# Attention parts in a written order on four engines: one change to the overlapped mLSTM and MLP kernel

## The chip, the cores and the metric

The kernel runs on one core of one Trainium2 chip. The metric is the device time of one execution in microseconds, the median of three runs. The profile is of one further execution. Engine names: PE is TensorE, ACT is ScalarE, DVE is VectorE, POOL is GpSimd, and SP is the engine whose queue triggers the DMAs.

## The reference, cut to what matters

An mLSTM layer (4 batches, 8 heads, 768 positions, head size 40) is followed by two two-layer MLPs over the same 3072 tokens (320 to 2048 to 320), the first with a squared ReLU, the second with SiLU. Everything is float32.

```python
for t in range(S):
    m_new = np.maximum(f_gate[:, :, t] + m, i_gate[:, :, t])
    f_stab = np.exp(f_gate[:, :, t] + m - m_new)
    i_stab = np.exp(i_gate[:, :, t] - m_new)
    C = f_stab * C + i_stab * np.einsum('bhd,bhe->bhde', vt, kt)
    n = f_stab * n + i_stab * kt
    h_tilde = np.einsum('bhde,bhe->bhd', C, qt)
    y[:, :, t] = sigmoid(o_gate) * h_tilde / np.maximum(np.abs(n . qt), 1.0)
x = relu(y @ w1_in) ** 2 @ w1_out
h = x @ w2_in
out = (h * sigmoid(h)) @ w2_out
```

## The kernel before

**Attention.** The recurrence is done in chunks of 128 positions, all 8 heads together. One chunk of one batch is a *tile*, and there are 24, numbered i. Tiles 0 to 5 use a simpler form (`i < N_NAT`); the others split their numbers into parts that TensorE multiplies exactly. A tile's work: `load_a`, `load_w`, `load_e` start the DMAs (q and k, v, the decay matrix W, the row factors eq); `SK` copies q and k on ACT into `tt`, `SK2` subtracts on DVE and issues nine DMAs `stk<-tt` (lines 286 and 288) that stack the parts on partitions; `WT` masks W on POOL and takes its exponentials on ACT, eight ACTIVATEs; `SC(i, hf)` multiplies q and k for one half of the heads on PE into a PSUM tile, then multiplies by W and makes the parts p1, p2, p3 on DVE (lines 320, 326, 327); `QT` scales q and splits it into qh (ACT) and ql (DVE); `VK` splits v and k on DVE; `HG` is the output product on PE, 48 small matmuls and nine for the carried state; `EV` normalises it on DVE; `ST` makes the new state on PE, then adds and splits it on DVE and ACT (`cs`); `xt` transposes the result on PE and writes x on ACT (line 467) and DVE (line 468).

**MLP one** runs over blocks of 384 tokens, three tiles each, eight blocks. A block has 16 steps (`KF`). Step j does `emit_in` for step j+3 (8 matmuls `hin`, line 530, then relu and two squares on ACT, lines 537, 538, 540, and later `gl` on DVE, line 549) and `emit_out` for step j (8 matmuls into three PSUM tiles). The PSUM tiles of `hin` are two, so the `hin` of one step needs the relu of the one two earlier. After step 15 the block's output goes through `ob` (ACT, DVE, ACT, lines 573 to 575) and a DMA (line 576) to DRAM. MLP two is alike and has no attention beside it.

**Overlap.** The attention tiles of block n+1 are done during block n (and the last six steps of the one before). `plan(i)` gives every part of tile i a moment in steps, relative to `b = base(i)`, the start of its score product; three tiles are 5.33 steps apart, at 10, 15.33 and 20.67 counted from the start of a block. A moment is rounded down to half a step: `run_events(slot)` emits the parts of the first half between `emit_in` and `emit_out`, those of the second half after `emit_out`. In the same places the weights of MLP two are decoded (`w_load`, `w_dec`, then a store to DRAM), one of 16 pieces every six steps. Raw weights, decoded weights and `ob` share two buffers with the tag `raw`.

**Order.** PE executes in the order in which the code emits. For ACT, DVE, POOL and the SP queue the order is found by a scheduler, which takes instructions as they come ready in its own model of time, and starts from the emitted order as a priority. Every engine and the queue then executes in the order given to it: an instruction that waits holds those behind it.

Of the kernel before, what the change touches and what calls it, by code (L numbers as in the profile page):

```python
# [22 lines left out]
L = 128  # L23
# [37 lines left out]
def mlstm_moe_kernel(  # L61
# [104 lines left out]
    def w_split(raw, which, layer, u, pl):  # L166
# [3 lines left out]
        act.activation(out=f(t), in_=f(hi), func=ACTF.Prelu, scale=2.0 ** -112, alpha=-2.0 ** 32)  # L170
        dve.tensor_scalar(out=t, in0=t, scalar1=3, scalar2=None, op0=ALU.logical_shift_left)
        dve.scalar_tensor_tensor(out=t, in0=lo, scalar=29, in1=t,
                                 op0=ALU.logical_shift_right, op1=ALU.bitwise_or)
        if which == "i":
# [7 lines left out]
            act.activation(out=w[:, 0:3], in_=tv, func=ACTF.Copy)  # L182
            eng = pool if layer == 1 else dve
            eng.tensor_tensor(out=w[:, 3:5], in0=tv[:, 0:2], in1=f(w[:, 0:2]), op=ALU.subtract)
            eng.tensor_tensor(out=w[64:128, 2], in0=tv[64:128, 2], in1=f(w[64:128, 2]), op=ALU.subtract)
        else:
            if layer == 1:
                w = wp.tile([128, 2, 640], F32R, tag=f"wo{u}", name=f"wo{u}")
                wout[layer, u] = w
            else:  # L190
                ws = pl.tile([128, 1280], F32R, tag="raw", name="ws")
                w = ws.rearrange("p (j n) -> p j n", j=2)
            tv = f(t).rearrange("p (j n) -> p j n", j=2)
            if layer == 1:
                for c, oh, ol in ((slice(0, 256), slice(0, 256), slice(256, 512)),
                                  (slice(256, 320), slice(512, 576), slice(576, 640))):
                    act.activation(out=w[:, :, oh], in_=tv[:, :, c], func=ACTF.Copy)
                    pool.tensor_tensor(out=w[:, :, ol], in0=tv[:, :, c], in1=f(w[:, :, oh]), op=ALU.subtract)
                return
            oh, ol = w[:, :, 0:320], w[:, :, 320:640]  # L200
            act.activation(out=oh, in_=tv, func=ACTF.Copy)
            dve.tensor_tensor(out=ol, in0=tv, in1=f(oh), op=ALU.subtract)
        if layer == 2:
            raws["st", which, u] = lambda: sp.dma_start(out=w2_d[which, u], in_=f(ws))
# [20 lines left out]
    def load_a(i):  # L225
# [12 lines left out]
        v = d["vk"] = at.tile([128, DM + 2 * VW], F32, tag="vk", name="vk", bufs=2)  # L238
        sp.dma_start(out=v[:, 0:DM + VW], in_=vk[i * L:(i + 1) * L])

    def load_s(n):
        t0, nt = blk_tiles[n]
        sg = T["sg", n] = at.tile([128, 3, DM], F32, tag="sg", name="sg", bufs=1)
        sp.dma_start(out=sg[:, 0:nt], in_=og[t0 * L:(t0 + nt) * L].rearrange("(k p) f -> p k f", p=L))
        act.activation(out=sg[:, 0:nt], in_=sg[:, 0:nt], func=ACTF.Sigmoid)
# [45 lines left out]
    def WT(i, hf):  # L291
        b, c = TILES[i]
        w = T[i]["W", hf]
        pool.affine_select(out=w, in_=w, pattern=[[0, 4], [1, L]], compare_op=ALU.is_ge,  # L294
                           fill=NEG, base=0, channel_multiplier=-1)
        r0 = b * H + 4 * hf
        for h in range(4):
            act.activation(out=w[:, h], in_=w[:, h], func=ACTF.Exp, bias=aw[:, 0, c, r0 + h:r0 + h + 1])  # L298

    def SC(i, hf):  # L300
# [5 lines left out]
        for h in range(4):  # L306
            if i < N_NAT:
# [6 lines left out]
                      start=True, stop=True)  # L314
        w = d["W", hf]
# [12 lines left out]

    def VK(i):
        b, c = TILES[i]  # L330
        d = T[i]
        vkt = d["vk"]
        k, v, r = vkt[:, 0:DM], vkt[:, DM:DM + VW], vkt[:, DM + VW:DM + 2 * VW]
# [5 lines left out]
        dve.tensor_tensor(out=r, in0=v, in1=top(v), op=ALU.subtract)  # L339
        v3 = at.tile([128, VW], BF16, tag="v3", name="v3", bufs=2)  # L340
        dve.tensor_tensor(out=v3, in0=r, in1=top(r), op=ALU.subtract)
        d["v"] = [x.rearrange("p (h c) -> p h c", c=42) for x in (top(v), top(r), v3)]
# [13 lines left out]
    def QT(i):  # L356
# [6 lines left out]
        (pool if i < N_NAT else dve).tensor_tensor(out=q, in0=q, in1=eqv(i)[0:120], op=ALU.mult)  # L363
        if i < N_NAT:
            return
        act.activation(out=qh[0:120], in_=q, func=ACTF.Copy)
        dve.tensor_tensor(out=ql[0:120], in0=q, in1=f(qh[0:120]), op=ALU.subtract)
# [50 lines left out]
    def ST(i):  # L418
# [3 lines left out]
        cv = cc2[b % 2][0:120]  # L422
        cs = cs2[b % 2][0:120]
        mv = bmask[0:120, 0:H].to_broadcast([120, H, 42])

        def grow(h0, h1, m, src):
            dve.scalar_tensor_tensor(out=cv[0:m, h0:h1], in0=cv[0:m, h0:h1],
                                     scalar=eqv(i)[0:m, h0 // 3, L - 1:L], in1=src, op0=ALU.mult, op1=ALU.add)

        ps = p_at.tile([128, 512], F32, tag="at", name="st")[:, 0:VW].rearrange("p (h c) -> p h c", c=42)  # L430
        if i < N_NAT:
            vkt = T[i]["vk"]
            ks, vp, pairs = [vkt], [vkt[:, DM:DM + VW].rearrange("p (h c) -> p h c", c=42)], ((0, 0),)
        else:
            ks, vp, pairs = T[i]["k"], T[i]["v"], PAIRS
        for h in (0, 3, 6):
            n = min(3, H - h)
            for m, (x, y) in enumerate(pairs):
                pe.matmul(ps[0:40 * n, h:h + n], ks[x][:, 40 * h:40 * h + 40 * n], vp[y][:, h:h + n],
                          start=m == 0, stop=m == len(pairs) - 1)  # L440
        if c == 0:
            act.activation(out=cv[:, 0:6], in_=ps[0:120, 0:6], func=ACTF.Copy)
            act.activation(out=cv[0:80, 6:8], in_=ps[0:80, 6:8], func=ACTF.Copy)
        else:
            for h in (0, 3, 6):
                n = min(3, H - h)
                grow(h, h + n, 40 * n, ps[0:40 * n, h:h + n])
# [350 lines left out]
```

## Time and profile before

| what | us |
|---|---|
| median of 3 runs | 919.86 |
| the three runs | 915.72, 919.86, 926.69 |
| the profiled execution | 918.51 |
| its span, first to last instruction | 916.8 |
| PE busy in the span | 860.2 |
| DVE busy | 513.4 |
| ACT busy | 515.5 |

PE is busy nearly all the time, ACT and DVE a little over half. A busy PE is not one at its peak, since matmuls overlap. The first `emit_out` of the eight blocks of MLP one starts at 74.3, 152.5, 220.7, 282.3, 344.5, 408.4, 472.7 and 525.2 us; MLP two begins near 570. Blocks two to seven, the ones in the change's name, are 152.5 to 525.2.

### The profile page before, as it was taken

To read this page: it belongs to the slowest core of one execution; us is meant where nothing else is said; L and a number is where in the kernel's file an instruction comes from. 1 tells how busy PE (TensorE), PEld (TensorE's weight loads), DVE (VectorE), ACT (ScalarE), POOL (GpSimd) and SP (SyncE) were. 2 spreads that over 40 slices of the span, in tenths; PEclk is the share of its full clock that TensorE was granted. 3 is DMA by queue.
4 is the path that set the end of the run, shared out by engine and by line. 5 is a ranking of instruction groups with operands and counts; after the bars stand their busy time and mean duration, and the time that the engine had idled before them with its cause. 6 is when DMAs were issued, how large, how long until landed. Compare 5 with 4: busy or idle time off the path is not lost.

```text
span 916.8 us, 15812 instructions
## 1 busy us (share of the span) xinstructions
PE 860.2 (94%) x5964; PEld 839.9 (92%) x5964; DVE 513.4 (56%) x1001; ACT 515.5 (56%) x1071; POOL 94.6 (10%) x121
## 2 busy tenths in 40 slices
PE   3868979898899899899999999999999999999998
PEld 3758979898899899899999999999999999999998
DVE  5576476866656877778666323443444444444443
ACT  3677556766686686768675655343434344343343
POOL 4675200000000100000000000000000000000000
PEclk9997999989999999999899999999999999999999
DMA  8794355656846647657444477010101010000000
GB/s 244 240 281 151 108 168 166 231 157 182 247 147 205 208 124 253 196 170 243 146 135 151 144 247 248 11 57 1 57 1 56 1 57 1 23 1 22 1 22 23
DMA packets 72582, 117.50 MB, mean 128 GB/s; under 512 B 5306, under 2 KB 54394, under 8 KB 72266
## 3 DMA queue, kind: packets, MB, share of 16 engines
q1 hardware_dynamic: 72506, 116.50, 40.3%
q8 instruction: 47, 0.77, 0.4%
q14 instruction: 29, 0.24, 0.1%
HBM read 77.23 MB, written 19.33 MB: 105 GB/s over the span
## 4 chain that ended last, share of the span: by engine, by line
PE 62%; DMA 15%; ACT 8%; DVE 7%; SPq 4%; issue 2%; POOL 1%; POOLq 0%; ACTq 0%; DVEq 0%
PE hin L530 29%; DMA W<-g_d 8%; PE o L582 6%; PE o L580 6%; PE o L581 6%; ACT W L298 3%; DMA eq<-e_d 3%; PE o L563 2%; PE o L565 2%; PE o L564 2%; SPq L288 2%; PE hA L401 2%; DVE gl L549 1%; DMA stk<-tt 1%; PE o L568 1%
## 5 line engine op out<-in xcount | busy, mean ns | idle before, releaser
L530 PE MATMUL hin<-x,wi 128*128 128x384 f32 x2048 | 417.5, 346 | 14.7 <-ACT r L537 7.6
L530 PEld LDWEIGHTS hin<-x,wi 128*128 128x128 f32 x2048 | 366.1, 192 | 19.9 <-ACT r L537 10.1
L549 DVE TENSOR_TENSOR gl<-r,gh 128x384 fp32r<-128x384 f32 x256 | 147.3, 577 | 131.1 <-ACT gh L546 68.9
L545 DVE TENSOR_TENSOR r<-hin,r 128x384 f32<-128x384 f32 x128 | 71.4, 558 | 121.9 <-ACT r L544 121.8
L544 ACT ACTIVATE r<-hin 128x384 f32<-128x384 f32 x128 | 63.0, 492 | 131.7 <-PE hin L530 131.6
L582 PE MATMUL o<-wo,gl 128*128 128x320 f32 x384 | 118.7, 309 | 0.0
L580 PE MATMUL o<-wo,gh 128*128 128x320 f32 x384 | 118.3, 308 | 0.0
L581 PE MATMUL o<-wo,gh 128*128 128x320 f32 x384 | 117.8, 307 | 0.0
L546 ACT ACTIVATE gh<-r 128x384 fp32r<-128x384 f32 x128 | 67.3, 526 | 73.9 <-DVE r L545 73.9
L563 PE MATMUL o<-gh,wo 128*128 128x384 f32 x256 | 91.8, 359 | 3.9 <-ACT ob L573 3.9
L565 PE MATMUL o<-gl,wo 128*128 128x384 f32 x256 | 87.5, 342 | 2.3 <-DVE gl L549 2.3
L537 ACT ACTIVATE r<-hin 128x384 f32<-128x384 f32 x128 | 61.6, 481 | 48.7 <-PE hin L530 48.4
L564 PE MATMUL o<-gh,wo 128*128 128x384 f32 x256 | 87.6, 342 | 0.0
L581 PEld LDWEIGHTS o<-wo,gh 128*128 128x128 f32 x384 | 72.1, 188 | 0.0
L580 PEld LDWEIGHTS o<-wo,gh 128*128 128x128 f32 x384 | 72.1, 188 | 0.0
L582 PEld LDWEIGHTS o<-wo,gl 128*128 128x128 f32 x384 | 72.0, 187 | 0.0
L294 POOL TENSOR_SCALAR_AFFINE_SELECT W<-W 128x512 f32<-128x512 f32 x48 | 35.7, 768 | 346.8 <-DMA W<-g_d 129.9
L298 ACT ACTIVATE W<-W,aw 128x128 f32<-128x128 f32 x192 | 60.9, 390 | 18.0 <-POOL W L294 17.9
L538 ACT ACTIVATE gh<-r 128x384 fp32r<-128x384 f32 x128 | 67.0, 524 | 2.7
L540 ACT ACTIVATE r<-r 128x384 f32<-128x384 f32 x128 | 66.8, 522 | 2.6
L563 PEld LDWEIGHTS o<-gh,wo 128*128 128x128 f32 x256 | 49.6, 194 | 5.5 <-ACT ob L573 4.3
L565 PEld LDWEIGHTS o<-gl,wo 128*128 128x128 f32 x256 | 49.0, 191 | 3.0 <-DVE gl L549 3.0
(124 smaller groups left out, 1191.6 us busy)
## 6 DMA issues: line engine op xcount, KB each, us to landing
stk<-tt SPq DMA_DIRECT2D x162, 120.0 KB
raw<-in_w_in_dram SPq DMA_DIRECT2D x16, 768.0 KB
W<-g_d SPq DMA_DIRECT2D x24, 512.0 KB
raw<-in_w_out_dram SPq DMA_DIRECT2D x16, 640.0 KB
vk<-in_vk_dram SPq DMA_DIRECT2D x24, 328.0 KB
rqk<-in_qk_dram SPq DMA_DIRECT2D x18, 360.0 KB
w2i_d<-ws SPq DMA_DIRECT2D x8, 640.0 KB
w2o_d<-ws SPq DMA_DIRECT2D x8, 640.0 KB
```

The costliest lines, as they stand in the source:

```text
L298: act.activation(out=w[:, h], in_=w[:, h], func=ACTF.Exp, bias=aw[:, 0, c, r0 + h:r0 + h + 1])
L530: pe.matmul(ps[:, 0:N], w[:, c, ws], x[:, sl, 0:N], start=(k == 0), stop=(k == 7))
L538: act.activation(out=gh, in_=r, func=ACTF.Square)
L545: dve.tensor_tensor(out=g, in0=ps[:, 0:N], in1=r, op=ALU.mult)
L546: act.activation(out=gh, in_=g, func=ACTF.Copy)
L549: low.append(lambda: on("gl" if ly == 1 else "gl2", gi).tensor_tensor(out=gl, in0=g, in1=f(gh), op=ALU.subtract))
L563: pe.matmul(o[k][:, 0:N], w[:, c], gh, start=first, stop=False)
L564: pe.matmul(o[k][:, 0:N], w[:, c2], gh, start=False, stop=False)
L565: pe.matmul(o[k][:, 0:N], w[:, c], gl, start=False, stop=last)
L580: pe.matmul(o[k][:, 0:DM], gh[:, c], w[:, 0:320], start=first, stop=False)
L581: pe.matmul(o[k][:, 0:DM], gh[:, c], w[:, 320:640], start=False, stop=False)
L582: pe.matmul(o[k][:, 0:DM], gl[:, c], w[:, 0:320], start=False, stop=last)
```

## The change

`plan(i)` now has 26 parts where there were 14 (and the sigmoid load, which becomes two). Most functions that used two engines are divided: `load_a` into `load_q` and `load_v`, `WT` into `WT` (POOL) and `WE` (ACT), `SC` into `SC` (PE) and `SD` (DVE), `VK` into `VV` and `VK`, `QT` into `QT`, `QH`, `QL`, `ST` into `ST`, `GR`, `CH`, `CL`, and `xt` into `XT`, `XA`, `XL`. The weight decoding becomes a generator whose five pieces are called at five moments, after each tile's `b` instead of every six steps. From the start of block two to the start of block eight the emitted order holds for ACT, DVE and the SP queue as it does for PE; POOL keeps the scheduler's order. The instructions themselves are the same.

```diff
+    def WE(i, hf):
+        b, c = TILES[i]
+        w = T[i]["W", hf]
         r0 = b * H + 4 * hf
         for h in range(4):
             act.activation(out=w[:, h], in_=w[:, h], func=ACTF.Exp, bias=aw[:, 0, c, r0 + h:r0 + h + 1])
...
+    def SD(i, hf):
+        d = T[i]
+        ps = d["sc", hf]
...
         def plan(i):
             b = base(i)
             p = base(i - 2) if i >= nb0 + 2 else -20.0
-            todo = [(b - 6.3, lambda: load_a(i)), (max(b - 5.5, p + 3.6), lambda: load_w(i)),
-                    (max(b - 3.6, p + 4.8), lambda: load_e(i)), (b - 4.2, lambda: SK(i)), (b - 3.4, lambda: SK2(i)),
-                    (b - 2.0, lambda: (WT(i, 0), WT(i, 1))), (b - 0.4, lambda: VK(i)),
-                    (b, lambda: SC(i, 0)), (b + 0.5, lambda: SC(i, 1)), (b + 0.6, lambda: QT(i)),
-                    (b + 3.2, lambda: (HG(i, 0), HG(i, 1), HG(i, 2))), (b + 3.9, lambda: EV(i)),
-                    (b + 4.6, lambda: ST(i)), (b + 6.4, lambda: xt(i))]
+            e = KF * (i // 3) - AHEAD
+            q0 = max(b - 8.0, p + (1.2 if i < N_NAT else 2.4))
+            todo = [(q0, lambda: load_q(i)), (max(b - 5.0, p + 4.8), lambda: load_v(i)),
+                    (max(b - 6.4, p + 3.8), lambda: load_w(i)), (max(b - 4.6, p + 5.5), lambda: load_e(i)),
+                    (max(b - 4.4, q0 + 0.6), lambda: SK(i)), (max(b - 3.7, q0 + 1.2), lambda: SK2(i)),
+                    (b - 2.4, lambda: WT(i, 0)), (b - 2.3, lambda: WT(i, 1)),
+                    (b - 1.8, lambda: WE(i, 0)), (b - 1.2, lambda: WE(i, 1)), (b - 1.5, lambda: VV(i)),
+                    (b, lambda: SC(i, 0)), (b + 0.5, lambda: SD(i, 0)), (b + 0.9, lambda: QT(i)),
+                    (b + 1.0, lambda: SC(i, 1)), (b + 1.4, lambda: QH(i)), (b + 1.5, lambda: SD(i, 1)),
+                    (b + 2.2, lambda: QL(i)), (b + 2.6, lambda: VK(i)),
+                    (b + 3.3, lambda: (HG(i, 0), HG(i, 1), HG(i, 2))), (b + 3.9, lambda: EV(i)),
+                    (b + 4.4, lambda: ST(i)), (b + 4.9, lambda: GR(i)), (b + 5.4, lambda: CH(i)),
+                    (b + 6.1, lambda: CL(i)),
+                    (min(b + 6.1, e - 1.6), lambda: XT(i)), (min(b + 6.6, e - 1.1), lambda: XA(i)),
+                    (min(b + 6.9, e - 0.6), lambda: XL(i))]
             if i % 3 == 0:
-                todo.append((b - 1.0, lambda: load_s(i // 3)))
+                todo.append((b - 0.9, lambda: load_s(i // 3)))
+                todo.append((b + 1.5, lambda: sig(i // 3)))
...
-            for at_, fn in ((17.0, lambda e=e: w_load(2, e, stp)), (19.0, lambda e=e: w_dec(2, e, stp)),
-                            (21.5, lambda e=e: raws.pop(("st", *e))())):
-                events.setdefault(int(2 * (at_ + 6 * k)), []).append((at_ + 6 * k, fn))
+            dec = []
+            b = base(6 + k)
+            fns = [(b + 1.0, lambda e=e: w_load(2, e, stp)),
+                   (b + 3.0, lambda e=e, dec=dec: (dec.append(w_dec(2, e, stp)), next(dec[0])))]
+            fns += [(b + x, lambda dec=dec: next(dec[0], None)) for x in (3.6, 4.4, 5.1, 6.5)]
+            for at_, fn in fns:
+                events.setdefault(int(2 * at_), []).append((at_, fn))
...
-        with tc.manual_schedule(engines={nc.tensor.engine}):
+        with ExitStack() as order:
+            order.enter_context(tc.manual_schedule(engines={pe.engine}))
...
+                if ly == 1 and n in (1, nb1 - 1):
+                    order.close()
+                    order.enter_context(tc.manual_schedule(
+                        engines={pe.engine, act.engine, dve.engine, sp.engine} if n == 1 else {pe.engine}))
```

## Rows read from the trace of the kernel before

**Rows 1.** Busy time by stretch: blocks one to eight of MLP one, each from its first `emit_out` to the next block's. Columns: stretch and its length, busy us (and instructions) of PE, PE's weight loads, DVE, ACT and POOL, mean granted PE clock, DMA share, GB/s.

```profile
74.30:152.50 78.20, 72.06 (x477) 68.06 (x476) 47.26 (x101) 48.77 (x107) 17.30 (x19) 0.93 0.43 131
...
282.30:344.50 62.20, 58.96 (x507) 56.33 (x506) 46.41 (x100) 44.20 (x99) 4.74 (x6) 1.00 0.61 186
344.50:408.40 63.90, 60.73 (x518) 59.25 (x516) 48.33 (x107) 45.25 (x98) 4.17 (x6) 0.97 0.62 201
408.40:472.70 64.30, 62.12 (x518) 60.67 (x515) 46.39 (x101) 44.82 (x98) 4.58 (x6) 0.95 0.56 181
220.70:282.30 61.60, 57.91 (x470) 55.98 (x470) 42.96 (x87) 45.40 (x99) 4.45 (x6) 0.97 0.60 186
152.50:220.70 68.20, 61.89 (x515) 60.15 (x515) 47.50 (x104) 45.80 (x100) 4.42 (x6) 0.95 0.61 199
472.70:525.20 52.50, 51.74 (x387) 50.35 (x386) 28.93 (x57) 31.53 (x62) 2.12 (x2) 1.00 0.45 149
525.20:570.00 44.80, 44.80 (x258) 44.17 (x257) 12.63 (x22) 26.24 (x49) 1.02 (x1) 1.00 0.77 245
```

**Rows 2.** The waits of blocks two to seven (152.5 to 525.2 us): who waited for whom, us in total, times, the longest.

```profile
ACT tt L274 <- DMA stk<-tt: 36.8, 13, 5.3
...
PEld L401 <- DVE p L327: 9.6, 6, 2.4
...
PE hA L401 <- DVE p L327: 8.9, 6, 2.3
PEld hin L530 <- ACT r L537: 7.1, 7, 3.2
...
PE hin L530 <- ACT r L537: 5.3, 5, 2.9
PEld o L563 <- ACT ob L573: 4.3, 2, 3.7
...
PE o L563 <- ACT ob L573: 3.9, 2, 3.5
...
PEld o L565 <- DVE gl L549: 1.6, 1, 1.6
...
PE o L565 <- DVE gl L549: 1.3, 1, 1.3
```

**Rows 3.** ACT in order of time, a piece of block three. Columns: start us, us, engine, line, operation, output and input, count, and in brackets the idle time before it and what ended it.

```profile
244.61 2.45 ACT L298 ACTIVATE W<-W,aw 128x128 f32<-128x128 f32 x8 [3.29 <-POOL W L294]
246.96 0.47 ACT L537 ACTIVATE r<-hin 128x384 f32<-128x384 f32 x1
```

**Rows 4.** DVE, and in the last row PE, in order of time around the output product of tile 17 in block five.

```profile
372.58 0.69 DVE L326 TENSOR_TENSOR pr<-W 128x512 f32<-128x512 f32 x1
373.18 0.95 DVE L172 SCALAR_TENSOR_TENSOR dt<-raw,dt 128x768 int32<-128x768 int32 x1
374.05 0.56 DVE L549 TENSOR_TENSOR gl<-r,gh 128x384 fp32r<-128x384 f32 x1
374.52 0.69 DVE L327 TENSOR_TENSOR p<-pr 128x512 bf16<-128x512 f32 x1
...
375.26 0.19 PE L401 MATMUL hA<-vk,p 128*128 128x42 bf16 x1 [2.32 <-DVE p L327]
```

**Rows 5.** The stacking DMAs of two tiles on the SP queue (first of nine triggers), and the ACT copy of the next tile, which waited for the last of them to land.

```profile
322.90 0.86 SPq L286 DMA_DIRECT2D stk<-tt  x1
...
332.56 0.84 ACT L274 ACTIVATE tt<-rqk 120x768 fp32r<-120x768 f32 x1 [1.61 <-DMA stk<-tt]
...
342.99 0.88 SPq L286 DMA_DIRECT2D stk<-tt  x1
...
355.22 0.85 ACT L274 ACTIVATE tt<-rqk 120x768 fp32r<-120x768 f32 x1 [2.76 <-DMA stk<-tt]
```

**Rows 6.** PE in order of time: an `emit_out` and an `emit_in` without attention (366.36, 367.77 and the start of what follows); an output product `HG` from its first matmul to the next `emit_out` (331.58, 333.84); a state product `ST` to the next `emit_in` (356.76, 357.68).

```profile
331.58 0.23 PE L395 MATMUL hA<-cs,qh 120*128 120x126 f32 x1
...
333.84 0.42 PE L563 MATMUL o<-gh,wo 128*128 128x384 f32 x1
...
356.76 0.22 PE L439 MATMUL st<-vk,k 128*120 128x126 bf16 x1
...
357.68 0.60 PE L530 MATMUL hin<-x,wi 128*128 128x384 f32 x2
...
366.36 0.34 PE L563 MATMUL o<-gh,wo 128*128 128x384 f32 x1
...
367.77 1.55 PE L530 MATMUL hin<-x,wi 128*128 128x384 f32 x8
369.15 0.34 PE L563 MATMUL o<-gh,wo 128*128 128x384 f32 x1
```

**Rows 7.** The DVE subtraction of `SK2` in blocks two to seven: line, operation, shapes, count, busy us and mean ns of one, idle time before them.

```profile
L284 DVE TENSOR_TENSOR tt<-rqk,tt 120x768 fp32r<-120x768 f32 x15 | 14.4, 958 | 39.4 <-ACT tt L274 36.4 <-DMA eq<-e_d 2.3 <-DMA w2i_d<-ws 0.7
```

**Rows 8.** The SP queue in order of time: a store of decoded weights to DRAM and the load that waited for it to land; behind them a row of the queue's waits from 343 to 372 us.

```profile
358.86 0.33 SPq L204 DMA_DIRECT2D w2i_d<-ws  x1
...
362.11 0.33 SPq L158 DMA_DIRECT2D raw<-in_w_in_dram  x1
...
SPq L158 <- DMA w2i_d<-ws: 1.2, 1, 1.2
```

**Rows 9.** The longest wait of PE for x in block one (74.3 to 152.5 us).

```profile
PE hin L530 <- ACT x L467: 3.1, 1, 3.1
```

More of the change, by code (lines that the diff above doesn't have):

```diff
@@ L185, in w_split @@
             eng.tensor_tensor(out=w[64:128, 2], in0=tv[64:128, 2], in1=f(w[64:128, 2]), op=ALU.subtract)
-        else:
[L187 to L192, printed above, removed]
-            tv = f(t).rearrange("p (j n) -> p j n", j=2)
[L194 to L199, printed above, removed]
+        elif layer == 1:
+            w = wp.tile([128, 2, 640], F32R, tag=f"wo{u}", name=f"wo{u}")
+            wout[layer, u] = w
+            tv = f(t).rearrange("p (j n) -> p j n", j=2)
+            parts = ((slice(0, 256), slice(0, 256), slice(256, 512)),
+                     (slice(256, 320), slice(512, 576), slice(576, 640)))
+            for c, oh, ol in parts:
+                act.activation(out=w[:, :, oh], in_=tv[:, :, c], func=ACTF.Copy)
+            yield
+            for c, oh, ol in parts:
+                pool.tensor_tensor(out=w[:, :, ol], in0=tv[:, :, c], in1=f(w[:, :, oh]), op=ALU.subtract)
+        else:
+            ws = pl.tile([128, 1280], F32R, tag="raw", name="ws")
+            w = ws.rearrange("p (j n) -> p j n", j=2)
+            tv = f(t).rearrange("p (j n) -> p j n", j=2)
             oh, ol = w[:, :, 0:320], w[:, :, 320:640]
             act.activation(out=oh, in_=tv, func=ACTF.Copy)
+            yield
             dve.tensor_tensor(out=ol, in0=tv, in1=f(oh), op=ALU.subtract)
         if layer == 2:
-            raws["st", which, u] = lambda: sp.dma_start(out=w2_d[which, u], in_=f(ws))
+            yield
+            sp.dma_start(out=w2_d[which, u], in_=f(ws))
     def w2_take(which, u):
@@ L237, in load_a, with load_v @@
             d["q"] = r[:, 1]
-        v = d["vk"] = at.tile([128, DM + 2 * VW], F32, tag="vk", name="vk", bufs=2)
+    def load_v(i):
+        v = T[i]["vk"] = at.tile([128, DM + 2 * VW], F32, tag="vk", name="vk", bufs=2)
         sp.dma_start(out=v[:, 0:DM + VW], in_=vk[i * L:(i + 1) * L])
+    def load_a(i):
+        load_q(i)
+        load_v(i)
     def load_s(n):
@@ L327, in SC, with VV @@
         on(f"p3{hf}", i).tensor_tensor(out=p3, in0=r, in1=d["p2", hf], op=ALU.subtract)
+    def VV(i):
+        d = T[i]
+        if i < N_NAT:
+            return
+        vkt = d["vk"]
+        v, r = vkt[:, DM:DM + VW], vkt[:, DM + VW:DM + 2 * VW]
+        dve.tensor_tensor(out=r, in0=v, in1=top(v), op=ALU.subtract)
+        v3 = at.tile([128, VW], BF16, tag="v3", name="v3", bufs=2)
+        dve.tensor_tensor(out=v3, in0=r, in1=top(r), op=ALU.subtract)
+        d["v"] = [x.rearrange("p (h c) -> p h c", c=42) for x in (top(v), top(r), v3)]
     def VK(i):
@@ L338, in VK @@
             return
[L339 to L342, printed above, removed]
         if c < NC - 1:
@@ L360, in QT, with QH, QL @@
         q = d["q"][0:120].rearrange("p (g t) -> p g t", g=3)
-        qh = d["qh"] = at.tile([128, 3, L], F32R, tag="qh", name="qh")
-        ql = d["ql"] = at.tile([128, 3, L], F32R, tag="ql", name="ql")
[L363 to L367, printed above, removed]
+        (pool if i < N_NAT else dve).tensor_tensor(out=q, in0=q, in1=eqv(i)[0:120], op=ALU.mult)
+    def QH(i):
+        d = T[i]
+        if TILES[i][1] == 0 or i < N_NAT:
+            return
+        q = d["q"][0:120].rearrange("p (g t) -> p g t", g=3)
+        qh = d["qh"] = at.tile([128, 3, L], F32R, tag="qh", name="qh")
+        act.activation(out=qh[0:120], in_=q, func=ACTF.Copy)
+    def QL(i):
+        d = T[i]
+        if TILES[i][1] == 0 or i < N_NAT:
+            return
+        q = d["q"][0:120].rearrange("p (g t) -> p g t", g=3)
+        ql = d["ql"] = at.tile([128, 3, L], F32R, tag="ql", name="ql")
+        dve.tensor_tensor(out=ql[0:120], in0=q, in1=f(d["qh"][0:120]), op=ALU.subtract)
     def HG(i, g):
@@ L440, in ST, with GR @@
                           start=m == 0, stop=m == len(pairs) - 1)
+    def GR(i):
+        b, c = TILES[i]
+        if c == NC - 1:
+            return
+        d = T[i]
+        ps = d["st"]
+        cv = cc2[b % 2][0:120]
+        mv = bmask[0:120, 0:H].to_broadcast([120, H, 42])
         if c == 0:
@@ L483, in xt @@
             XT(i)
+            XA(i)
+            XL(i)
     def steps(i):
@@ L615, in mlstm_moe_kernel @@
         load_s(0)
+        sig(0)
         consts()
@@ L622, in mlstm_moe_kernel @@
         SK2(0)
-        WT(0, 0)
-        WT(0, 1)
+        for hf in range(2):
+            WT(0, hf)
+            WE(0, hf)
         gate_stack.close()
@@ L639, in w_dec @@
         def w_dec(layer, e, pl):
-            k, u = e
-            w_split(raws.pop((layer, e)), k, layer, u, pl)
+            return w_split(raws.pop((layer, e)), e[0], layer, e[1], pl)
         nw = [0, 0]
@@ L649, in w_upto @@
                     nw[1] += 1
-                w_dec(1, wq[nw[0]], stp)
+                for _ in w_dec(1, wq[nw[0]], stp):
+                    pass
                 nw[0] += 1
```

61 lines of the change are left out of this document (36 added, 25 removed).

## The prediction

> **What bounds the kernel now.** I read the stretches block by block first. In block eight, where no attention runs beside the MLP, PE is busy for all of its 44.8 us at the full clock; in blocks two to seven it is busy 51.7 to 62.1 us of 52.5 to 68.2, and in four of them the mean granted clock is below 1.00 [rows 1]. So PE is the bound, DVE with 29 to 48 us and ACT with 32 to 46 us have room, and what can be gained is what PE loses: idle time and time at the lower clock. I put both in numbers before I looked at causes.
>
> Idle time: in blocks two to seven PE's matmuls waited 8.9 us for p3 of the score product, 5.3 for a relu, 3.9 for `ob` and 1.3 for gl, together 19.4 us; the weight loads in front of them waited 9.6 + 7.1 + 4.3 + 1.6 = 22.6 us for the same [rows 2]. I take the middle, 21 us.
>
> Clock: a mean of 0.95 means that part of the stretch ran at 1.2 GHz and not 2.4; what is lost is (1 - clock) times the length, if PE had work in it. That is 0.05 x 68.2 + 0.03 x 61.6 + 0.03 x 63.9 + 0.05 x 64.3 = 10.3 us [rows 1]. The longest single waits of PE are 2.3 to 3.5 us [rows 2]; I take 10 us for the clock and treat it as hanging on them. Recoverable in all: 31 us of the 918.5 us of the profiled execution.
>
> Then the causes, from the waits and the order of time. They are of one kind: something is far ahead in an engine's order and waits, and what PE needs stands behind it. ACT waited 36.8 us in `SK` for the stacking DMAs of the tile before [rows 2]; in block three it waited 3.29 us for the mask of W, then did eight exponentials in 2.45 us, and only then the relu that PE was waiting for [rows 3]. In block five DVE put a weight-decoding step of 0.95 us and a gl between the last two operations for p3, while PE waited 2.32 us [rows 4]. These engines have a quarter of their time free; the order is at fault, not the amount.
>
> **The change part by part.** No instruction is added or taken away, so PE's own work stays. Four things move.
>
> *ACT's and DVE's order.* `WE` follows PE at b - 1.8 and b - 1.2 in two pieces of four exponentials, where the eight now stand together; `SK` comes at b - 4.4. A step without attention takes 1.41 + 1.38 = 2.8 us on PE [rows 6]. The stacking DMAs of the tile before are planned for b - 9.0; they take 9.7 to 12.2 us from first trigger to landing [rows 5], at most four and a half steps of 2.8 us and less in steps with attention, so that they land by about b - 5 and `SK` no longer waits. W is loaded at b - 6.4 and masked from b - 2.4, four steps later. So the waits of [rows 2, 3] have no ground any more. `VK` and the decoding's DVE part move behind the score product, and between `SD` of the second half (b + 1.5) and `HG` (b + 3.3) stands little: the stall of [rows 4] goes. I take the whole 21 us and 10 us off here and put back what is late next.
>
> *What is late next, first: the stacking.* This is the price I worked on longest. `stk` has one buffer, so its DMAs may start only when `SC` of the second half of the tile before is done, and that half moves from b + 0.5 to b + 1.0. And `SK2`, which they need, now stands on DVE behind that half's three operations and `XL`. From the end of that `SC` to the landing: three operations at 0.60 us each (372.58 to 373.18 is one) [rows 4], `XL` about 0.5, `SK2` 0.96 [rows 7], 3.3 us in all; then 9.7 to 12.2 us [rows 5]: 13.0 to 15.5 us. PE's time from there to the next `SC`, by the rounded moments, for the tile that starts at 15.33: an `emit_out` of 1.41 us, three steps of 2.8, an `HG` of 2.26, an `ST` of 0.92 and an `emit_in` of 1.38 [rows 6], 14.3 us. For the other two tiles of a block it is four and a half steps, 12.5 + 2.26 + 0.92 = 15.7 us. In one of these (20.67) the copy of `ob` and a decoding subtraction stand ahead on DVE, which I estimate at 1.2 us more: 14.2 to 16.7 against 15.7. The wait is then -1.3 to 1.2, -1.5 to 1.0 and about -2.4 to 0 us, and it can't be below nothing. I take 0.6, 0.4 and 0.1, as the middle of the leg lies at the edge of the room: 1.1 us a block of three tiles, and with 17 tiles 6 us. Its bounds are 0 and 13 us (2.2 us times 17/3).
>
> *Second: ql before `HG`.* `QL` stands on DVE behind `SK2`: 3.3 us, a gl and itself, each 0.5, 4.3 us after that `SC`; `HG` comes an `emit_out`, a step and an `emit_in` after it, 5.6 us [rows 6]. Room 1.3 us. I take 0.2 us a tile, 3.5 us; bounds 0 and 1 us a tile, 17 us.
>
> *The queue.* Each of its DMAs keeps its written place, so a trigger that waits holds the others. The worst place is the block's end: the store of `ob`, three eq triggers (at 0.8 us, as I estimate from the 0.86 and 0.88 of the stacking ones [rows 5]), a raw load whose buffer `ob` held, a store, then nine stacking DMAs. A store of 640 KB was followed 3.25 us later by the load that waited for it [rows 8]. With that I estimate the queue free some 2.7 us after the `SC` in question, before DVE is done with `SK2` (4.5 us): nothing. The smaller of PE's two waits for `ob` is 0.4 us (3.9 less 3.5) [rows 2]; I leave that in at every block end, 2 us for six.
>
> *POOL* keeps its freedom, and has only the masks. *Clock*: waits of a microsecond don't come near those that went before the drops; 1 us, bounds 0 and 10. *Block one* keeps the scheduler's order but gets the new priorities; the last transpose comes 0.8 step earlier, where PE waited 3.1 us for x [rows 9]. I take half of that, 1.5 us, between a loss of 4 and a gain of 5. MLP two is untouched.
>
> Sum: 31 + 1.5 - 6 - 3.5 - 2 - 1 = 20 us. 918.5 - 20 = 898.5 us. The profiled execution lies 1.4 us under the median of the runs shown, and those lie up to 11 us apart, so I leave the number as it is.
>
> **The rivals.** *The queue holds (slower).* The leg through the stacking DMAs is the loop of one tile to the next: if it takes longer than PE's work, it sets the pace. The mean room is (14.3 + 15.7 + 15.7)/3 = 15.2 us. From a mean leg of 15.2 + 31/17 = 17.0 us on, the change loses. Were DVE a step late (2.8 us) and the triggers spread by other DMAs as in the second case of [rows 5], the leg would be 3.3 + 2.8 + 12.2 = 18.3; at 18 us PE waits 2.8 x 17 = 48 us, and the time is 918.5 + 48 - 31 - 1.5 = 934 us. For it: there is no slack by design in any of the three places. Against: the lower end of the leg, 13.0, and that a late PE gives the leg more room by itself. The Trainium skill (Perfetto Trace Analysis, section DMA Instruction, HWDGE) says that a DMA's semaphore comes only after its write is confirmed, and that this "can cause a surprisingly long delay especially when the write target is HBM": by that the load behind the store of `ob` would hold the queue. The 3.25 us of [rows 8] do not show it long here; each microsecond over 5 would be one more in six places.
>
> *A wait takes the place of another.* In the written order DVE is late by 1 us at most parts: `HG` waits 0.7 us a tile for ql (12 us), the stacking 8, block ends 3, the clock 2. The gain is 31 - 25 = 6 and, with 1.5 for block one, 911 us. For it: DVE has 43 to 48 us of work in a block where PE is busy 58 to 62 [rows 1]. Against: that work is spread, and gl has two steps to spare.
>
> *The order is not another one.* If the scheduler's order were already near the written one, nothing moves: 918 us. Against it stands the 36.8 us of `SK` [rows 2], which a part at b - 4.4 would not show.
>
> **How the numbers follow.** A measurement of this kernel tells about 1% from no change. Forecast (884 to 908): 0.68. Wait for wait (908 to 917): 0.13. The queue (over 920): 0.12. No other order: 0.07. The lower end of the range is all of the 31 us and a gain of 3.5 in block one, 918.5 - 34.5 = 884. The upper end, 917, takes in the second case; what lies above, the third and the fourth, is under 0.2. Faster by over 1% means under 910.7: the forecast and 0.05 of the second case, 0.73. Within 1%: the rest of the second, the fourth and none of the third, 0.15. Slower: 0.12.
>
> **What would show it.** Right: blocks three to six at 58 to 60 us instead of 61.6 to 64.3, granted clock 1.00 in them, no wait of `SK` for stacking DMAs, no wait of `HG` for p3 over 1 us. The first return would be PE at the score product waiting for the stacking DMAs, mostly at the tile that starts at 15.33, the second `HG` waiting for ql. Wrong: waits over 1 us at the score product of every tile (the queue), or ACT waiting in `WE`, `QH` or the decoding with a relu behind it, which would make blocks as long as now.

## The result and the profile after

The changed kernel takes 888.37 us (median of four runs, 887.66 to 893.13); the kernel before takes 919.15 us (median of four, 915.72 to 926.69). The ratio is 0.967, with a 95% interval of 0.960 to 0.973: faster by about 31 us. The profiled execution took 887.66 us, with a span of 885.9, against 918.51 and 916.8 before, 30.9 us less.

Where the time went is read first by stretch. These are blocks one to seven of MLP one in the changed kernel, with the columns of [rows 1]:

```profile
73.80:145.50 71.70, 67.86 (x477) 64.94 (x476) 49.85 (x101) 48.04 (x105) 22.04 (x23) 0.98 0.53 162
145.50:204.30 58.80, 58.80 (x517) 57.86 (x516) 50.61 (x104) 48.41 (x100) 5.20 (x6) 1.00 0.68 207
204.30:261.30 57.00, 55.71 (x471) 54.63 (x471) 42.68 (x84) 45.80 (x97) 4.32 (x7) 1.00 0.70 220
261.30:324.70 63.40, 59.98 (x507) 58.30 (x507) 51.82 (x103) 47.17 (x101) 4.89 (x7) 0.97 0.66 202
324.70:384.50 59.80, 59.00 (x516) 57.86 (x516) 52.61 (x107) 47.17 (x99) 6.18 (x8) 1.00 0.70 214
384.50:443.20 58.70, 58.70 (x516) 57.78 (x515) 51.70 (x105) 47.04 (x99) 4.35 (x7) 1.00 0.72 217
443.20:494.30 51.10, 51.10 (x386) 50.34 (x385) 27.43 (x52) 31.34 (x65) 2.73 (x3) 1.00 0.34 106
```

Against [rows 1], blocks two to seven go from 372.7 to 348.8 us (-23.9) and block one from 78.2 to 71.7 (-6.5); the start is 0.5 us shorter, and from the start of block eight to the end both kernels take 391.6 us. In three of these six blocks PE is now busy from end to end, and of the six only block four has a granted clock below 1.00.

These are the waits of blocks two to seven (145.5 to 494.3 us), first of PE, its weight loads and ACT, then of the DMA queue:

```profile
PE sc L331 <- DMA stk<-tt: 5.3, 5, 2.2
...
PEld hA L436 <- DVE ql L406: 0.5, 2, 0.3
...
ACT dt L170 <- DMA raw<-in_w_in_dram: 4.9, 2, 2.6
...
SPq L303 <- DVE tt L299: 38.6, 16, 4.3
SPq L636 <- DVE ob L634: 23.9, 6, 5.4
```

In [rows 2] PE's matmuls waited for p3, a relu, `ob` and gl, 19.4 us in all, and ACT stood 36.8 us in `SK` for the stacking DMAs. All five are gone. One kind of wait of PE's matmuls is left, at the score product, for those same stacking DMAs: five waits, 5.3 us in all. Two of them are at tile 14, shown next; the other three are at tiles 11, 16 and 17:

```profile
220.86 0.41 PE L331 MATMUL sc<-stk 120*128 120x128 f32 x2 [1.29 <-DMA stk<-tt]
...
320.78 0.44 PE L331 MATMUL sc<-stk 120*128 120x128 f32 x2 [0.90 <-DMA stk<-tt]
...
341.69 0.41 PE L331 MATMUL sc<-stk 120*128 120x128 f32 x2 [0.68 <-DMA stk<-tt]
```

The queue now does the standing, in line 303 for the subtraction of `SK2` and in line 636 for `ob`.

The worst of the four tiles is tile 14, in block four. First the queue in order of time at the end of block three, then DVE's subtraction, then PE, with the columns of [rows 5]:

```profile
261.00 0.60 SPq L636 DMA_DIRECT2D x_d<-ob  x1
261.70 0.57 SPq L247 DMA_DIRECT2D vk<-in_vk_dram  x1
262.31 2.35 SPq L275 DMA_DIRECT2D eq<-e_d  x3
264.77 0.78 SPq L163 DMA_DIRECT2D raw<-in_w_out_dram  x1
265.60 0.43 SPq L210 DMA_DIRECT2D w2i_d<-ws  x1
266.13 0.89 SPq L301 DMA_DIRECT2D stk<-tt  x1
...
273.14 1.50 SPq L303 DMA_DIRECT2D stk<-tt  x2
...
266.44 0.95 DVE L299 TENSOR_TENSOR tt<-rqk,tt 120x768 fp32r<-120x768 f32 x1
...
276.69 0.30 PE L331 MATMUL sc<-stk 120*128 120x128 f32 x1 [0.25 <-DMA stk<-tt]
279.18 0.41 PE L331 MATMUL sc<-stk 120*128 120x128 f32 x2 [2.19 <-DMA stk<-tt]
```

The score product that frees `stk` is over where block four begins: PE's next instruction starts at 261.22, and what is said below to come so long after a score product is counted from that start. The queue has just been let go by `ob` (it stood 5.4 us for it) and has seven triggers to give before the first stacking one: from 261.00 to 266.13. The last stacking trigger ends at 274.6, and PE gets its data at 279.2, after waits of 0.25 and 2.19 us. The 0.97 of block four follows that wait.

### The profile page after: what moved, and what is told of

The parts are those of the page before. It is cut to its first block, busy times and chain, and to the rows that moved or that the text cites. A ratio compares the mean times of both kernels' runs of the same rounds, so it can differ in the third digit from the quotient of the medians.

```text
span 885.9 us, 15802 instructions
## 1 busy us (share of the span) xinstructions
PE 846.0 (95%) x5964; PEld 830.2 (94%) x5964; DVE 532.1 (60%) x1001; ACT 522.3 (59%) x1071; POOL 96.4 (11%) x121
## 4 chain that ended last, share of the span: by engine, by line
PE 79%; DMA 12%; ACT 4%; SPq 3%; DVE 2%; issue 1%; POOL 0%; POOLq 0%; ACTq 0%; DVEq 0%
PE hin L590 36%; PE o L642 6%; PE o L640 6%; PE o L641 6%; PE o L623 4%; PE o L624 4%; PE o L625 4%; DMA stk<-tt 2%; DMA sg<-in_og_dram 2%; DMA w2o_d<-ws 2%; PE o L628 2%; PE hA L440 2%; PE o L630 2%; PE st L471 1%; DMA eq<-e_d 1%; DMA x_d<-ob 1%
## 5 line engine op out<-in xcount | busy, mean ns | idle before, releaser
L590 PE MATMUL hin<-x,wi 128*128 128x384 f32 x2048 | 409.8, 342 | 5.8 <-ACT r L597 2.9
L308 POOL TENSOR_SCALAR_AFFINE_SELECT W<-W 128x512 f32<-128x512 f32 x48 | 38.8, 832 | 318.4 <-DMA W<-g_d 118.8
L623 PEld LDWEIGHTS o<-gh,wo 128*128 128x128 f32 x256 | 48.8, 191 | 0.2
L624 PEld LDWEIGHTS o<-gh,wo 128*128 128x128 f32 x256 | 48.8, 190 | 0.0
```

What stands on the lines that cost most here:

```text
L590: pe.matmul(ps[:, 0:N], w[:, c, ws], x[:, sl, 0:N], start=(k == 0), stop=(k == 7))
L623: pe.matmul(o[k][:, 0:N], w[:, c], gh, start=first, stop=False)
L624: pe.matmul(o[k][:, 0:N], w[:, c2], gh, start=False, stop=False)
```

## The experiments

Each ratio is to runs of the kernel before on the same chip (medians 920.73, 917.54 and 920.55 us in the three groups of runs). The new plan has 28 parts, as the diff of the change counts them, not 26. "Blocks" below means blocks two to seven of the profiled execution: 372.7 us before, 348.8 after.

**Plan or order.** The changed plan and divided parts, with the written order on PE alone:

```diff
-                        engines={pe.engine, act.engine, dve.engine, sp.engine} if n == 1 else {pe.engine}))
+                        engines={pe.engine}))
```

> The new plan with all its divided parts, but the written order kept on PE alone, as before; ACT, DVE and the SP queue get the scheduler's order. If the written order on the engines is what removed PE's waits, blocks two to seven stay near the 372.7 us that they take before, block one keeps the 6.5 us that it gained after, and the time is 905 to 918 us. If the new moments and the finer parts are what did it, with any order that starts from them as priorities, the time is 885 to 895 us.

Measured: 926.37 us, ratio 1.006 (1.002 to 1.010), blocks 386.9, above both ranges. The waits of its blocks two to seven:

```profile
ACT tt L289 <- DMA stk<-tt: 36.8, 13, 5.1
...
PE hin L590 <- ACT r L597: 11.3, 8, 3.4
PE o L623 <- DVE ob L634: 9.3, 5, 2.9
PE hA L440 <- DVE p L350: 7.1, 5, 2.1
```

They are the waits of [rows 2] again, down to the 36.8 us of `SK` over 13 tiles. The emitted order changed in every line of the plan, and the order that the scheduler made out of it has the same waits. So the plan alone gives nothing.

The other half, the old plan and the undivided functions with the written order on four engines from block two to block eight:

```diff
-        with tc.manual_schedule(engines={nc.tensor.engine}):
+        with ExitStack() as order:
+            order.enter_context(tc.manual_schedule(engines={pe.engine}))
...
+                        engines={pe.engine, act.engine, dve.engine, sp.engine} if n == 1 else {pe.engine}))
```

> The kernel before with its old plan and undivided parts, and only the written order on ACT, DVE and the SP queue from block two to block seven. If order alone is the gain, blocks two to seven lose 24 us and the time is 890 to 900 us (block one has the old plan, so the 6.5 us there are missing). If the parts must be one-engine and spread for a written order to work, the undivided ones hold the engines: ACT waits for POOL twice in the mask and for DVE in the decoding with a relu behind it, 1 to 3 us a tile or more, and the time is 915 to 950 us.

Measured: 1009.65 us, ratio 1.097 (1.090 to 1.104), blocks 462.6, clock 0.947 over the span, slower than both ranges. Its waits:

```profile
ACT qh L366 <- DVE rqk L363: 73.1, 14, 7.1
DVE dt L171 <- ACT dt L170: 45.3, 14, 10.0
...
PE hin L530 <- ACT x L467: 28.2, 5, 9.2
```

An undivided function hands an intermediate from DVE to ACT inside one moment. In a strict order ACT stands at it until DVE has worked off its own list, 5 us a tile in `QT`, and what is behind it on ACT comes late, most of all x, for which PE waits 28.2 us (for a relu only 2.4). The order alone loses 9.7%, the plan alone nothing, both together gain 3.3%: the two halves of the change can't be priced apart. The plan is itself two things, divided functions and new moments, and no run has the whole of one without the other.

Was it the queue that lost there? The same kernel with the queue given back to the scheduler:

```diff
-                        engines={pe.engine, act.engine, dve.engine, sp.engine} if n == 1 else {pe.engine}))
+                        engines={pe.engine, act.engine, dve.engine} if n == 1 else {pe.engine}))
```

> The old plan with its undivided parts and the written order on PE, ACT and DVE, the SP queue free again; with the queue written too it took 1009.7 us. If the queue's order was that loss, the time is 900 to 930 us. If the undivided parts hold ACT and DVE (ACT waited 73 us in QT for DVE, DVE 45 us for ACT in the decoding), 950 to 1000 us remain.

Measured: 1000.81 us, ratio 1.088 (1.082 to 1.093), blocks 457.0, with 70.9 us of ACT at `qh` over 14 tiles: at the upper end of the range for undivided parts, a little past it. Under a tenth of the loss was the queue's. Then one function alone was divided in that kernel, `QT`, which held ACT longest:

```diff
...
+            if i >= 9:
+                todo += [(b + 1.9, lambda: QH(i)), (b + 2.4, lambda: QL(i))]
```

> The old plan with the written order on PE, ScalarE and VectorE, as f3 (1000.8 us), and of the 26 parts two alone: QT divided into its ScalarE part at 1.9 and its VectorE part at 2.4 us of the tile, for tiles from 9 on. Theory: in an undivided part a strict ScalarE stands for VectorE in the middle of it, and the 71 us that ScalarE stood at qh for rqk over 14 tiles is the main hold; then that wait falls under 15 us and the time is 955 to 975 us. Rival: the hold moves on to the next undivided part; then another wait of ScalarE or VectorE takes 30 to 60 us, PE's for x and r stay above 25 us, and the time is 985 to 1000 us.

Measured: 1004.30 us, ratio 1.091 (1.087 to 1.095), blocks 459.9. (The 1.9 and 2.4 of the expectation are steps, not us.) The wait in question fell nearly as far as the theory had it, and the time did not fall:

```profile
ACT r L551 <- PE hin L544: 104.2, 45, 8.2
...
ACT cs L468 <- DVE u L467: 22.4, 10, 4.2
...
ACT qh L374 <- DVE rqk L363: 17.7, 7, 5.5
PE hA L411 <- DVE ql L381: 16.9, 7, 5.1
```

From 70.9 to 17.7 us at `qh`, nothing gained. The rival held in that the hold moved on, though not in its figures. Of PE's waits the one for x fell from 29.4 us (ACT's and DVE's copies together) to 16.3, and the one for ql rose from 0.6 to 16.9; ACT, let go at `qh`, now waits for PE, 104.2 us where it was 42.2. The next undivided function on ACT, `cs`, held it 22.7 us before and 22.4 after. `QL` also went from b + 0.6 to b + 2.4 here, so the wait for ql may come from the moment and not from what is still undivided; no run tells. The longest wait of an engine in strict order was here no measure of what its removal brought.

**Which engine's order.** The changed plan with the written order on PE and ACT, and on PE and DVE (the queue is the scheduler's in both; with neither it is the first experiment, with both the one after these):

```diff
-                        engines={pe.engine, act.engine, dve.engine, sp.engine} if n == 1 else {pe.engine}))
+                        engines={pe.engine, act.engine} if n == 1 else {pe.engine}))
```

> The new plan with the written order kept by PE and ScalarE alone; VectorE and the DMA queue are the scheduler's. Neither of the two engines gave 926 us, both of them 882.6. Theory A, ScalarE carries it: the scheduler's ScalarE stood 36.8 us over 13 tiles at SK for the stacking DMAs, and everything behind it there came late; then this run is at 882 to 892 us, ScalarE's wait for stk gone, PE's waits for r and p with it. Theory B, VectorE carries as much: PE still waits for p and ob, 7 to 9 us each, and the time is 900 to 920 us.

> The new plan with the written order kept by PE and VectorE alone; ScalarE and the DMA queue are the scheduler's. Theory A, ScalarE carries it: its wait for stk stays at 30 to 40 us over 13 tiles, and the time is 910 to 926 us. Theory B, VectorE carries as much: 895 to 910 us, with PE's waits for p and ob under 3 us.

Measured: ACT 904.11 us, ratio 0.981 (0.977 to 0.986), blocks 362.7; DVE 953.28 us, ratio 1.035 (1.031 to 1.039), blocks 410.4. Neither theory foresaw the second. The first has the time of theory B and the waits of theory A: with ACT alone, the wait of `SK` for the stacking DMAs and PE's waits for r and p are gone, and PE waits for other things of DVE, ql (6.2 us) and x (4.4):

```profile
DVE vk L358 <- DMA vk<-in_vk_dram: 25.5, 14, 6.3
...
PE hA L436 <- DVE ql L406: 6.2, 3, 4.1
```

With DVE alone, the waits, and then one copy of `SK` on ACT in order of time:

```profile
DVE gl L609 <- ACT r L600: 111.8, 42, 6.5
...
ACT tt L289 <- DMA rqk<-in_qk_dram: 30.4, 10, 4.4
...
PE hA L436 <- DVE ql L406: 15.6, 5, 3.3
```

```profile
233.79 0.85 ACT L289 ACTIVATE tt<-rqk 120x768 fp32r<-120x768 f32 x1 [3.64 <-DMA rqk<-in_qk_dram]
```

The scheduler pulls `SK` forward on ACT until it stands for the load, the relu and the squares come late behind it, and a strict DVE can't pass the gl that needs them: it stands 111.8 us. ACT waits back for DVE in the decoding too, 27.7 us over 10 times, so the share that `SK` alone has in this is argued and not shown. So the written order on ACT is worth 22 us by itself, that on DVE costs 27 us by itself, and the two together gain 44. DVE in strict order paid for an ACT that kept another one; ACT in strict order gained beside a DVE that did, though less than with both.

**The queue.** The change with the queue alone given back to the scheduler:

```diff
-                        engines={pe.engine, act.engine, dve.engine, sp.engine} if n == 1 else {pe.engine}))
+                        engines={pe.engine, act.engine, dve.engine} if n == 1 else {pe.engine}))
```

> As the changed kernel, but the SP queue has the scheduler's order; PE, ACT and DVE keep the written one. If the queue's order is a cost (its waits hold the stacking DMAs for which PE waits 5.3 us), this is 3 to 6 us faster than after: 882 to 886 us. If it is a help, since the scheduler would put DMAs ahead that are not due, 890 to 905 us. If neither, 886 to 891 us.

Measured: 882.62 us, ratio 0.959 (0.954 to 0.964), the fastest of all. Busy time over its blocks two to seven (the columns of [rows 1], summed), the one wait that PE's matmuls have in them, and the queue in order of time at the end of block three:

```profile
sum 341.10, PE 340.72 PEld 334.81 DVE 272.61 ACT 267.02 POOL 25.17; mean PE 56.79 PEld 55.80 DVE 45.43 ACT 44.50 POOL 4.19
```

```profile
PE hA L436 <- DVE ql L406: 0.3, 1, 0.3
```

```profile
255.05 1.02 SPq L247 DMA_DIRECT2D vk<-in_vk_dram  x1
...
262.26 0.60 SPq L636 DMA_DIRECT2D x_d<-ob  x1
264.72 0.33 SPq L163 DMA_DIRECT2D raw<-in_w_out_dram  x1
265.22 2.51 SPq L301 DMA_DIRECT2D stk<-tt  x3
268.72 4.98 SPq L303 DMA_DIRECT2D stk<-tt  x6
```

PE is busy for 340.72 of 341.1 us. At the block end shown, the scheduler had put the vk load (255.05) and the eq loads (from 210.8) ahead of the store of `ob`, so that one trigger stands between store and stacking where the written order has six. The written order of the queue costs 7.7 us of blocks two to seven (348.8 less 341.1), 5.0 of them in block four, the block of tile 14 (63.4 us there, 58.4 here).

**What in the queue.** The prediction put the stacking leg's delay on DVE. First `SK2` was moved ahead for tiles 9 and later, subtraction and stacking DMAs together:

```diff
-                    (max(b - 4.4, q0 + 0.6), lambda: SK(i)), (max(b - 3.7, q0 + 1.2), lambda: SK2(i)),
+                    (max(b - 4.4, q0 + 0.6), lambda: SK(i)), (b - 4.36 if i >= 9 else max(b - 3.7, q0 + 1.2), lambda: SK2(i)),
```

> As the changed kernel, but the subtraction before the stacking DMAs and these DMAs stand at b - 4.36 instead of b - 3.7 (tiles 9 and up), ahead of the second half's three DVE operations. If those operations and the subtraction behind them are the leg for which PE waits at the score product, its 5.3 us and the clock drop after them (1.6 us) go: 881 to 885 us. If the queue sets it (the triggers themselves, the store of ob, the landing), at most 1 or 2 us go: 886 to 889 us.

Measured: 961.76 us, ratio 1.045 (1.039 to 1.051), blocks 423.0, far outside both ranges. Its waits from 200 to 560 us, and the queue in order of time around one piece of the decoding, then ACT's first instruction on it:

```profile
DVE dt L172 <- ACT dt L170: 102.2, 13, 11.1
ACT dt L170 <- DMA raw<-in_w_in_dram: 51.3, 6, 10.7
ACT dt L170 <- DMA raw<-in_w_out_dram: 50.1, 7, 10.4
```

```profile
297.22 1.52 SPq L303 DMA_DIRECT2D stk<-tt  x2
298.79 0.48 SPq L163 DMA_DIRECT2D raw<-in_w_out_dram  x1
...
303.63 0.77 ACT L170 ACTIVATE dt<-raw 128x640 f32<-128x640 f32 x1 [7.52 <-DMA raw<-in_w_out_dram]
```

The nine stacking triggers had passed the raw weight load, which is planned at b + 1.0. That load now came only after they were given, and the decoding on ACT, which PE doesn't wait for by itself, stood for it in 13 places, up to 10.7 us at a time, with relus behind it (PE's matmuls waited 15.8 us for these, and 12.7 for x). Undoing that, by putting the load at b + 0.9 and the last decoding piece, with its store, at b + 6.25, both ahead of the stacking again:

```diff
-            fns = [(b + 1.0, lambda e=e: w_load(2, e, stp)),
+            fns = [(b + (0.9 if k >= 2 else 1.0), lambda e=e: w_load(2, e, stp)),
...
-            fns += [(b + x, lambda dec=dec: next(dec[0], None)) for x in (3.6, 4.4, 5.1, 6.5)]
+            fns += [(b + x, lambda dec=dec: next(dec[0], None)) for x in (3.6, 4.4, 5.1, 6.25 if k >= 2 else 6.5)]
```

> The kernel with the subtraction and the stacking DMAs at b - 4.36, which took 961.8 us, with two small queue steps put back ahead of the nine stacking DMAs: the raw weight load at b + 0.9 and the store of decoded weights at b + 6.25 (from the third weight piece on). If the loss came from the raw load standing behind the stacking DMAs, so that ACT waited 101 us in the decoding with the relus behind it, the time falls to 880 to 890 us. If it came from DVE or the stacking itself being early, it stays at 950 to 965 us.

Measured: 891.76 us, ratio 0.971 (0.964 to 0.977), blocks 351.8, a little above the first range: 71 of the 74 us that the step had cost (423.0 less 348.8) came back by two places in a queue, which were moved together. PE's wait for `stk` is 7.8 us, five waits at tiles 11, 14, 17 and 20, no better than the change's 5.3. So the subtraction alone was moved, with the stacking DMAs, as a part `SX` of their own, left in their place:

```diff
-                    (max(b - 4.4, q0 + 0.6), lambda: SK(i)), (max(b - 3.7, q0 + 1.2), lambda: SK2(i)),
+                    (max(b - 4.4, q0 + 0.6), lambda: SK(i)), (b - 4.36 if i >= 9 else max(b - 3.7, q0 + 1.2), lambda: SK2(i)), (max(b - 3.7, q0 + 1.2), lambda: SX(i)),
```

> As the changed kernel; only the DVE subtraction of SK2 moves to b - 4.36 (tiles 9 and up), ahead of the three operations of the second half, and the nine stacking DMAs stay at b - 3.7. If DVE's place in the leg is what PE waits for at the score product (5.3 us and a clock drop of 1.6), the time is 880 to 884 us. If the queue's written order sets the leg, it stays at 886 to 890 us.

Measured: 886.60 us, ratio 0.964 (0.959 to 0.969), blocks 348.3, and

```profile
PE sc L337 <- DMA stk<-tt: 4.7, 4, 1.6
```

The subtraction now ends 0.9 to 2.8 us after the score product that frees `stk`, except 4.4 at tile 14 (3.7 to 6.2 in the change). The wait of 0.9 us at tile 16 is gone, where the queue was free at once and the subtraction was late. At tiles 11, 14 and 17 the four other waits stay, no shorter than before, and the first stacking trigger still comes 3.7 to 5.7 us after the score product. DVE's place is not what these three wait for. Last, with this, the vk and eq loads were put 0.3 and 0.6 steps earlier (steps of the plan, not the us of the expectation), ahead of the store of `ob`:

```diff
-            todo = [(q0, lambda: load_q(i)), (max(b - 5.0, p + 4.8), lambda: load_v(i)),
-                    (max(b - 6.4, p + 3.8), lambda: load_w(i)), (max(b - 4.6, p + 5.5), lambda: load_e(i)),
+            todo = [(q0, lambda: load_q(i)), (max(b - 5.3 if i >= 9 else b - 5.0, p + 4.8), lambda: load_v(i)),
+                    (max(b - 6.4, p + 3.8), lambda: load_w(i)), (max(b - 5.2, p + 5.4) if i >= 9 else max(b - 4.6, p + 5.5), lambda: load_e(i)),
```

> The subtraction of SK stands ahead as in f2, and for tiles from 9 on the written triggers of the vk and eq loads stand 0.3 and 0.6 us earlier, so that at a block's end they are ahead of the store of ob and not behind it. Theory: what is left of the stk wait (4.7 us over 4 tiles in f2) is the SP queue standing still for ob with five triggers behind it; then the first stacking triggers of the 20.67 tiles come 1.5 to 3 us sooner, PE's wait for stk in blocks two to seven falls to 0 to 2 us, and the time is 881 to 884 us. Rival: the nine triggers themselves and the landing after the last one set it, or the loads now ahead delay the ob store and what stands behind it by as much; then the wait stays at 4 to 6 us and the time is 885 to 888 us.

Measured: 883.93 us, ratio 0.960 (0.956 to 0.964), blocks 343.0:

```profile
PE sc L337 <- DMA stk<-tt: 1.4, 1, 1.4
...
SPq L163 <- DMA x_d<-ob: 8.0, 3, 2.7
```

```profile
263.13 0.57 SPq L642 DMA_DIRECT2D x_d<-ob  x1
266.43 0.34 SPq L163 DMA_DIRECT2D raw<-in_w_out_dram  x1
```

Three of the four waits are gone, those of tiles 11 and 17 and one of the two at tile 14. At 11 and 17 the first stacking trigger comes 3.2 to 3.3 us after the score product where it was 3.7 to 4.2. That is a gain of only 0.5 to 0.9 us, less than the 1.5 to 3 of the expectation; the last trigger ends 0.9 to 1.6 us earlier. What holds the triggers at these block ends is now the raw load, which waits about 2.7 us for the store of `ob` to land (the rows above are those of tile 14); both use a `raw` buffer. At tile 14 the first trigger still comes at 4.9 us (5.7 before): there the store itself starts 0.7 us after the score product, at tiles 11 and 17 it starts 1.0 us ahead of that point. The total agrees with the theory that the queue at the block's end is what is left of the wait. The store, the triggers behind it and the traffic around the landing were moved in one step, so their shares stay open.

**Block one.** It keeps the scheduler's order, and gained 6.5 us. The change, with the transposes of tiles 3 to 5 and their copies put back to b + 6.4:

```diff
-                    (min(b + 6.1, e - 1.6), lambda: XT(i)), (min(b + 6.6, e - 1.1), lambda: XA(i)),
-                    (min(b + 6.9, e - 0.6), lambda: XL(i))]
+                    (b + 6.4 if i < 6 else min(b + 6.1, e - 1.6), lambda: XT(i)),
+                    (b + 6.4 if i < 6 else min(b + 6.6, e - 1.1), lambda: XA(i)),
+                    (b + 6.4 if i < 6 else min(b + 6.9, e - 0.6), lambda: XL(i))]
```

> As the changed kernel, but for the tiles 3 to 5 of block one the transpose and its two copies keep the old moment b + 6.4, undivided. If the earlier transpose is what block one gained (78.2 to 71.7 us), block one takes 75 to 78 us and the time is 891 to 895 us. If it came from other moves, 887 to 890 us.

Measured: 892.56 us, ratio 0.970 (0.963 to 0.976), block one 74.8 us against 71.7, with 2.1 us of PE for a relu and 0.9 for x there. Other kernels with the whole new plan and the early transpose have 71.2 to 78.0 us in block one, though they differ from the change only in later blocks. Those with the old plan, four of them, have 77.7 to 78.7. So the new plan takes some time off block one as a rule, but the 3 us of the earlier transpose lie within the scatter, the 71.7 of the change lies near its lower end, and what made up the 6.5 stays open.

## Why the prediction was right, and where it was not

The forecast was 20 us, 898.5 us; 30.9 us came in the profiled execution. Its terms:

*What was recoverable: right.* The idle 21 us and the 10 us of the clock were taken off whole. PE's waits of [rows 2] and the wait of `SK` are all gone, and the loss by clock, made as in the prediction, is 0.03 x 63.4 = 1.9 us against 10.3. Right too was the cause, an order and not an amount of work: with the plan alone and the order left to the scheduler every one of these waits came back. What the prediction did not see is that the written order and the new plan need each other. It treated the order as a good in itself; alone it costs 89 us. Of its signs, blocks three to six at 58 to 60 us, it got two (59.8 and 58.7); block three came to 57.0, and block four, with tile 14, to 63.4 at a clock of 0.97.

*The stacking leg: right in size by luck, wrong in place and cause.* 6 us were put back; PE's matmuls wait 5.3 us. "Mostly at the tile that starts at 15.33" failed. The sum's 0.6, 0.4 and 0.1 us a tile are 3.4 us for the tiles at 15.33, 2.3 for those at 20.67 and 0.6 for those at 10; measured are 0.9 (tile 16), 4.4 (four waits, at tiles 11, 14 and 17) and nothing. The step that failed is the one on the queue: free "some 2.7 us after the `SC` in question, before DVE is done", and so "nothing". At those three tiles at 20.67 the first stacking trigger came 3.3 to 4.9 us after it, and the last ended at 12.8 to 13.4, against 10.2 to 12.3 at the other tiles from 9 on; one more, tile 20, ended at 13.2 and did not wait, while tile 17, with the same 16.0 us to the next score product, ended at 12.8 and did: the landing behind the last trigger counts too. At tile 14 seven triggers took 5.1 us, one of them the vk load, which the sum did not have. The priced mechanism, DVE late with `SK2`, was real (3.7 to 6.2 us where 3.3 was worked out), and it held tile 16; taking it away brought those 0.9 us and left the other waits, so that the total fell by 0.6. The size was right because two errors met: DVE's share was too large and the queue's was nothing.

*ql before `HG`: too dear.* 3.5 us put back; the weight loads waited 0.5 us for it, the matmuls not at all. The prediction's own sum had 1.3 us to spare and charged 0.2 a tile all the same.

*Block ends: too dear.* 2 us put back for `ob`, none there. With ACT's and DVE's order written, the two copies come when PE's tile is done; the queue waits for them, not PE.

*Clock:* 1 us put back, 1.9 measured, all after the wait of 2.2 us at tile 14; the blocks with shorter waits kept 1.00. That the clock hangs on the longest waits is not shown: in block three of the kernel before PE waited 2.9 us for a relu (247.48), and from 226 us to the block's end the granted clock was 1.00.

*Block one:* 1.5 us foreseen, 6.5 measured, of which a part may be scatter. This term, with 0.5 us of the start, makes 5.5 of the 10.9 us that the forecast was short. The terms put back make 4.8 more: 12.5 foreseen, 7.7 measured (5.3, 0.5 and 1.9). The last 0.6 us is not assigned.

*The rivals.* The queue that sets the pace (934 us) did not come to pass: of three tiles its triggers hold only the one at the block's end. That the written queue holds the stacking DMAs there is right; the run with the queue free (882.62) and the two small moves that led to 883.93 show it. The loss to 961.76 shows the written queue in another place, the raw load that ACT's decoding waits for. That one wait takes another's place (911 us) did not come either: `HG` waits 0.5 us in all for ql, and the block ends nothing. On the landing of a store, the Trainium skill (Perfetto Trace Analysis, section DMA Instruction, HWDGE) was weighed for this place: a semaphore comes only once the write is confirmed. The trace agrees where the load stands right behind the store of `ob`, with up to 2.7 us of waiting in the last experiment on the queue, and once in the change, 2.7 us at tile 8; at tiles 11, 14, 17 and 20 of the change the vk and eq triggers stood between and covered it. The rival that nothing is reordered is refuted by the waits that vanish.

## What to carry to other kernels

A written order on several engines and a plan made for it, with parts that use one engine each, were one change here: the plan without the order gave nothing (1.006), the order without the plan lost (1.097), and of one strict engine beside a free one DVE lost (1.035) while ACT kept about half of the gain (0.981). In a strict queue price every trigger that stands between a release and the DMA you care about, and every DMA that a moved step jumps over; if only the compute engines' order was wrong, leave the queue to the scheduler (882.62 against 888.37). When a model gets the size of a wait right, look whether it has the place right too: here the place showed that the cause was for the most part another.

## What the runs showed of the hardware

The last stacking data came to PE well after the last trigger: at tile 14 the trigger ended at 274.64 and PE went on at 279.18, 4.5 us later, longer than the store of [rows 8] took (3.25); at the other three tiles that waited it was 3.3 to 4.6 us. Triggers take the queue time of their own, about 0.8 us for each of the eq and the stacking ones; the nine of a tile were in no run given in less than 7.2 us. PE's granted clock is 0.97 in block four, behind the wait of 2.2 us, and 1.00 in blocks three and five, whose waits for the same DMAs were shorter. A longer wait alone did not bring it down: behind one of 2.3 us, at tile 17 of the run with the raw load ahead of the stacking, it stayed at 1.00.
